# A transformer block on one core: one batch's states loaded and turned ahead of the others, first products over six banks, and a new order of all steps

## The chip, the cores and the metric

The kernel runs on one core of one Trainium2 chip. The metric is the device time of one execution in microseconds (us); several runs are taken and their median is compared. Engines in this text: PE is the matmul engine (TensorE), DVE is VectorE, ACT is ScalarE, POOL is GpSimd, SP is SyncE, which here only issues DMAs.

## What is computed

Two blocks follow each other. The first is a block-recurrent cross attention between tokens `x` and states:

```python
# x: (B=8, H=8, S=512, D=64), state: (8, 8, Ns=32, 64)
scores  = scale * x @ state^T            # (8, 8, 512, 32)
xread   = softmax(scores) @ state        # (8, 8, 512, 64)
scores2 = scale * state @ x^T            # (8, 8, 32, 512)
sread   = softmax(scores2) @ x           # (8, 8, 32, 64)
attn    = concatenate([xread, sread], axis=2)      # (8, 8, 544, 64)
# the second block: attn as 4352 rows of 512
h  = attn_rows @ w_in                    # (4352, 2048)
sp = maximum(h, 0) + log1p(exp(-abs(h)))           # softplus
out = (h * erf(sp)) @ w_out              # (4352, 512)
```

`x` and `state` are float32. The two weights are read as pairs of 32-bit words (float64) and are turned into float32 on the chip.

## The kernel before

**Tiling.** Batches are worked one after the other, each with its 512 tokens, in two passes over the hidden width: pass A takes the first half of `d_ff` (1024 columns) and the first half of both weights, pass B the second half. The rows that come from the states (`sread`) of all batches are done together between the passes ("SA", "SB"). The hidden layer is not taken from `xread`: for each batch the states are multiplied with `w_in` first (`mixed`, steps A1m, A2m, ...; for the first batch `mixed_part`, steps n00 to n12), and the softmax weights `y` are multiplied with that product. From the second batch on, these products and those with `w_out` are done with seven products in place of eight, with sums on DVE (`hidden`, `chain`, `second_twice`, `inner`).

**The first batch** has steps of its own: `attention0` (x0 to x3 turn x on PE, s0 turns its states, q0 and q1 are its scores, tm, max, less, exp, sum, inv, norm, ta are the first softmax in two halves, big, wt, wz, wn, tw the second one, rd0 and rt0 read x with it), and `first_unit` (first products h0 to h7, each of 512 columns, with ACT's softplus h0s and copy h0c, an error function for two of them, h0e, a product on DVE, h0g; then second products o00 to o36, where the first digit is the group of rows and the second the pair of k). h0 to h7 go to PSUM banks k modulo 3; the second products to banks 3 + r modulo 3. PSUM has eight banks; scores, turned tiles and `mixed` use banks 6 and 7, `mixed` also 1 and 2.

**The other batches** go through `attention(b)`: x is loaded in a turned layout by sixteen loads of 64 KB (a1xq0 to a1xq7, two each), turned on DVE (a1tx), the scores (a1s) are sixteen products into banks 6 and 7, copied by ACT (a1c0, a1c1), and so on to y (a1ta). `sums_y(b)` makes y's sums on DVE (y11 to y14); A1f01 and what follows are the hidden products of `chain`.

**The states of batches 1 to 7** are loaded by POOL: a POOL copy ("hold", L486) waits for the first batch's softmax weights, and eight DMAs (`load_st`, L360, steps lst1 to lst8, one for each head) follow it. Two steps u0 and u1 (`turn_states`, L1041) turn them on PE, four and three tiles of 128 by 128, into banks that `attention0` used, and DVE copies them back (u0c, u1c). Everything that uses `st` stands behind that.

**The weights.** `w_in` comes in pieces i0 to i3 (two 512 KB loads each), `w_out` in o0 to o3; each is converted by two passes on ACT (a0, a1) and two on DVE (v0, v1).

**The order.** Every piece of work is a named step. A long string, `ORDER`, lists all names (2511 of them before) in the order in which they are issued, and `in_order` adds a dependency between each instruction and the one before it on the same engine. So each engine, and each DMA queue (SP's, POOL's), works strictly in the order of that string. An entry such as `~6*19` stands for 19 filler products into bank 6, which keep PE at work while it has nothing else:

```python
        if name[0] == "~":
            k, n = name[1:].split("*")
            issue(name, lambda: warm(bank[int(k)][:, 0:P], int(n)))
        else:
            issue(name, do.pop(name) if ORDER.split() else do[name])
    in_order(begun)
```

**Lines of the profile.** L423 fillers, L441 turning of x, L448 of the first states, L456 scores, L461 four turned tiles (tm, ta, tw), L945 n00 to n12, L956 h0 to h7, L977 second products of the first batch, L524 and L534 rd and rt, L549 a1s, L638 A1m, L687 hidden products, L740 and L810 second products, L238, L239, L240 DVE's add, subtract and multiply, L246 copies and other steps that are called with arguments.

Of the kernel before, what the change touches and what calls it, by code (L numbers as in the profile page):

```python
# [20 lines left out]
warm lx0 lx1 lst0 lx2 lx3 i0l0 i1l1 i1l0 i0l1 x0 x1 x0c i2l0 s0 x1c x2 s0c i2l1 q0 x2c x3 q00c  # L21
i3l1 q01c i0a0 big0 tm0 x3c i0v0 i0a1 q1 i3l0 max0 q10c i0v1 q11c less0 a1xq6 ~7*5 tm1 i1a1 big1
n00 max1 exp0 i0+a0 less1 sum0 exp1 a1xq2 n00c0 sum1 i0+a1 i1a0 inv0 inv1 norm1 i2a0 norm0 hold
~6*19 ta1 i1v0 lst1 i2a1 ta0 n00c1 lst6 i0+v0 i1v1 lst3 ta1c lst2 ta0c i0+v1 lst7 i3a0 o1l0 ~0*6
n02 i2v0 lst4 n01 big n02c0 lst8 i2v1 i3a1 ~2*3 h0 lst5 n01c1 o0l1 n01c0 i3v0 wt0 o0l0 n02c1 n10
wt1 a1xq3 i3v1 h1 n10c0 o1l1 n10c1 a1xq0 y01 wz n12 h0s wn1 h0c u1 n12c1 h1s u0 u1c n12c0 h1c wn0
a1xq4 tw1 y02 u0c tw0 h0e a1xq1 h2 tw1c h0g a1xq5 tw0c o0a0 rd0 a1xq7 o1a0 o0v0 o3l0 h4 rn0 y04
o1v0 yl0 a1tx1 rt0 o3l1 h3 h2s a1tx0 h2c a1tx2 o1a1 a1tx3 h5 o0a1 o1v1 rc0 h4c o0v1 a1s h4s h3c h7
T1 h3s a2xq4 a1c0 a1c1 t01 o2l0 a1tu0 h5c a2xq3 h6 h5s a1my0 h7c t0k a1mx0 h7s a2xq1 a1tu1 o10 h6s
a1my1 a2xq0 a1mx1 a2xq2 A1m a1sb0 h2e t31 a1x0 a1sb1 a2xq7 h2g o20 a1ex0 a1x2 t02 a1ex1 a1sm0 a1x1  # L30
A1m10 o22 o2l1 a1sm1 A1m01 A1m11 a1iz y03 a1ey0 a1nm0 o12 a1nm1 A1m00 h6c a1ta0 o3a0 A1M1 A1f01
a1ta1 a1ey1 o00 y11 A1M2 A1f0c y12 a1ty0 A1f06 a1ty1 h4e A1f02 y13 a1kz A1M3 A1f0u2 a1x3 A1f05 y14
o2a1 a2xq6 h4g A1f07 o2a0 a2xq5 o02 t32 A1M4 A1f0u3 o2v0 A1f0c11 A1f0c22 A1f04 h6e o3v0 a1z0 A1f11
o3a1 a1z3 o2v1 a1z1 A1f03 a1z2 A1f0c21 yl1 a2tx0 o04 A1f1c o3v1 A1f16 A1f0c12 A1f0s12 A1f12 T2
A1f0s22 A1f1u2 rd1 A1f0s21 t11 a1iy A1f0s11 t04 A1f17 h6g a2x3 rn10 rn11 A1f1c11 rt1 A1f15 A1f1u3
t34 rc1 T4 A1f14 o24 A1f1c22 A1e0 t61 a2tx2 A1f13 t21 t41 a2s A1f1c12 A1f1s22 t22 o06 A1g0 A1f1s11
a3xq1 a2c1 t1k A1f1c21 o14 a2c0 A1f1s12 a2tu0 o0c A1f1s21 o16 o0d t12 a2mx0 a2x2 a3xq7 A1e1 a2my0
o30 t3k yk0 a2sb0 a3xq5 o26 a3xq2 A1g1 a2ex0 a3xq0 A2m a3xq4 a2sm0 a2x0 o32 A2m00 t62 a3xq3 a2iz
A2m10 t42 a2nm0 A2m11 t2k o2c o34 a3xq6 a2ey0 A2M1 A2m01 a2ta0 a2x1 a2ey1 o36 A2M2 y21 A1q A2f01
o3c A2f05 A2f0c a2ty0 o1c y22 A1ap50 A1A1 A2f06 y23 A1ap10 a2ty1 A2f0u2 A2M3 A2f02 a2kz a2iy y24  # L40
A2f07 t24 T3 A1ap11 A2f0u3 A2f0c11 A1A3 A1ap51 A1ac A2f04 A2f0c22 A2M4 A2f11 A2f0c21 a2z3 t33 t4k
A2f03 t03 A2f1c a2z2 t51 a2z0 a3tx2 A1ap20 a2z1 yk1 A2f16 A2f0c12 o2d A2f0s12 o3d A1A2 A2f12
A2f1u2 o1d A2f0s22 yl2 A2f15 t13 yk2 A2f1c11 t23 A2f17 t6k a3tx0 rd2 A2f1u3 A1A4 A2f14 rn21 a3x2
rn20 t52 A1b2 rt2 A1ap21 rc2 A2f1c22 a3s A1ac11 A1a2 A2f13 a3c0 a4xq3 t43 t64 A2f1c21 A1ap60 A1a3
a3c1 a4xq2 A1ap61 A2f1c12 a3x0 A1bp10 t5k a3tu0 A1au2 a4xq0 A2f1s12 A1bp11 A2f0s21 t14 A1ap70 a3x1
a3mx0 A2f1s21 a3x3 A1ap71 A2f1s11 a4xq6 A1a4 A2f1s22 A3m A2f0s11 a4xq7 t44 A1au3 a3sb0 a4xq5
A1ap40 A1ac22 a3ex0 A1ap41 a3my0 A1ap30 A1ac21 t63 a3sm0 A1bc A1ap31 A3m01 A3m11 A1bp60 A1b3 a3ey1
A1bp61 a3iz A1ac12 A3m10 A1bp20 a3ey0 a3nm0 A1d2 A1bp50 A1bu2 a4xq4 A3m00 t53 A1bp51 a3ta0 A1bp21
A1bp70 t54 A2e0 y31 A1bp71 A3M1 A3f01 a3ty1 A3f05 a3ty0 A1bu3 A3f0c A3M2 A1bp40 a3kz A2e1 y32
# [1101 lines left out]
```

## Time and profile before

| | |
|---|---|
| median of 3 runs | 689.32 us (688.62 to 690.2) |
| the profiled execution, its own time | 691.2 us |
| its span, first to last instruction | 689.1 us |
| mean granted TensorE clock | 0.994 |
| PE busy | 678.0 us (98%), 5569 instructions |
| DVE busy | 590.7 us (86%) |
| ACT busy | 489.5 us (71%) |
| POOL busy | 89.0 us (13%) |
| DMA | 87.15 MB, mean 126 GB/s |

The span is what the instructions of the core take in that one execution; its own time also holds what lies around them. Times in the trace count from the span's start. Busy times of engines overlap. A granted clock of 0.5 means that PE ran at half speed.

### The profile page before, as it was taken

The numbers are of one execution on the slowest core, as the hardware profiler recorded it, in microseconds if no ns is written. First come the engines' busy times: TensorE is split into PE (matmuls) and PEld (weight loads), VectorE is DVE, ScalarE is ACT, GpSimd is POOL, SyncE is SP. The second block draws the span as 40 slices with busy tenths as digits, with TensorE's granted clock in tenths as the row PEclk, the third lists the DMA queues.
The fourth block names the chain that finished last, engine by engine and source line by source line (L and its number), as shares of the span: only waits on it lengthen the run. The fifth ranks groups of instructions, "written<-read, shape, count | busy, mean of one in ns | idle before, by whom it ended". The sixth has DMA issues, their size and how long they took to land.

```text
span 689.1 us, 13808 instructions
## 1 busy us (share of the span) xinstructions
PE 678.0 (98%) x5569; PEld 588.7 (85%) x5569; DVE 590.7 (86%) x771; ACT 489.5 (71%) x763; POOL 89.0 (13%) x84
## 2 busy tenths in 40 slices
PE   9799999999999999999999999999999999999997
PEld 7436568989898898899998879898989898998996
DVE  6689999999999999999986689787968795968784
ACT  5799967968787776876785795757586838676721
POOL 0300000030021202020201012010202011101112
PEclk9899999999999999999999999999999999999999
DMA  9967367578779977696797335142323315141427
GB/s 297 208 166 181 95 160 232 144 113 194 171 119 245 158 176 134 146 258 139 177 237 170 89 86 71 68 65 53 46 70 44 72 17 100 18 68 16 78 54 123
DMA packets 145567, 87.15 MB, mean 126 GB/s; under 512 B 92512, under 2 KB 137824, under 8 KB 145504
## 3 DMA queue, kind: packets, MB, share of 16 engines
q1 hardware_dynamic: 126448, 67.72, 36.0%
q0 software_dynamic: 18512, 18.03, 20.9%
q8 instruction: 44, 0.72, 0.4%
q10 hardware_dynamic: 544, 0.52, 0.2%
q14 instruction: 19, 0.16, 0.1%
HBM read 46.14 MB, written 40.11 MB: 125 GB/s over the span
## 4 chain that ended last, share of the span: by engine, by line
PE 94%; DVE 2%; DMA 2%; ACT 1%; POOL 1%; issue 0%; DVEq 0%
PE b L810 47%; PE b L687 27%; PE b L740 5%; PE b L638 4%; PE b L1017 4%; PE b L977 3%; PE b L956 2%; DMA st<-in_state_dram 1%; PE b L524 1%; PE b L549 1%; POOL st L360 1%; DMA big<-in_x_dram 1%; PE b L1041 0%; PE b L461 0%; DVE ring L239 0%; DVE z L574 0%
## 5 line engine op out<-in xcount | busy, mean ns | idle before, releaser
L718 POOL DMA_DIRECT2D out_dram<-res x67 | 80.1, 1330 | 572.6 <-DVE res L238 179.7
L810 PE MATMUL b<-big,ring 128*128 128x128 f32 x1196 | 151.4, 275 | 0.0
L810 PEld LDWEIGHTS b<-big,ring 128*128 128x128 f32 x1196 | 144.9, 192 | 4.0 <-ACT res L246 1.0
L246 ACT COPY ring<-b 128x512 f32<-128x512 f32 (+1 forms) x144 | 82.7, 584 | 89.4 <-PE b L687 64.8
L687 PE MATMUL b<-y,m 128*128 128x256 f32 x480 | 121.3, 381 | 0.2 <-DVE y L246 0.2
L246 ACT COPY res<-b 128x512 f32<-128x512 f32 (+2 forms) x125 | 64.4, 524 | 53.9 <-PE b L810 37.3
L687 PEld LDWEIGHTS b<-y,m 128*128 128x128 f32 x480 | 86.5, 190 | 12.9 <-ACT ring L246 1.5
L687 PE MATMUL b<-sy,m 128*128 128x256 f32 x360 | 91.9, 380 | 0.0
L240 DVE TENSOR_TENSOR ring<-ring 128x2048 f32<-128x2048 f32 (+1 forms) x36 | 77.8, 2166 | 9.3 <-ACT ring L695 8.2
L676 ACT ACTIVATE ring<-ring 128x512 f32<-128x512 f32 x128 | 77.0, 632 | 1.0 <-DVE ring L238 0.5
L687 PEld LDWEIGHTS b<-sy,m 128*128 128x128 f32 x360 | 65.0, 190 | 9.0 <-issue 1.1
L810 PEld LDWEIGHTS b<-ta,ring 128*128 128x128 f32 x548 | 67.8, 192 | 5.5 <-issue 3.4
L810 PEld LDWEIGHTS b<-big,ta 128*128 128x128 f32 x572 | 68.9, 192 | 3.4 <-ACT res L246 1.7
L810 PE MATMUL b<-big,ta 128*128 128x128 f32 x572 | 71.8, 275 | 0.0
L810 PE MATMUL b<-ta,ring 128*128 128x128 f32 x548 | 71.8, 276 | 0.0
L239 DVE TENSOR_TENSOR ring<-ring 128x1024 f32<-128x1024 f32 (+3 forms) x66 | 68.8, 1046 | 0.1
L238 DVE TENSOR_TENSOR ring<-ring,b 128x512 f32<-128x512 f32 (+1 forms) x72 | 47.1, 658 | 25.3 <-PE b L687 8.7
L695 ACT ACTIVATE ring<-ring 128x2048 f32<-128x2048 f32 x30 | 57.4, 1913 | 0.2
L238 DVE TENSOR_TENSOR res<-res,b 128x512 f32<-128x512 f32 (+2 forms) x60 | 35.9, 599 | 24.2 <-PE b L810 14.3
L246 ACT COPY b<-b 128x512 f32<-128x512 f32 (+2 forms) x63 | 34.4, 548 | 16.6 <-PE b L810 12.3
L238 DVE TENSOR_TENSOR res<-res 128x512 f32<-128x512 f32 (+1 forms) x56 | 42.0, 751 | 0.8
L238 DVE TENSOR_TENSOR ring<-ring 128x1024 f32<-128x1024 f32 (+1 forms) x35 | 39.8, 1141 | 0.2
(143 smaller groups left out, 972.0 us busy)
## 6 DMA issues: line engine op xcount, KB each, us to landing
out_dram<-res POOLq DMA_DIRECT2D x63, 256.0 KB, 4.8
out_dram<-res SPq DMA_DIRECT2D x32, 256.0 KB, 3.0
big<-in_x_dram SPq DMA_DIRECT2D x30, 256.0 KB, 4.1
big<-in_x_dram SPq DMA_DIRECT2D x112, 64.0 KB, 3.1
big<-in_moe_w_in_dram SPq DMA_DIRECT2D x12, 512.0 KB, 5.4
...
```

What stands on the lines that cost most here:

```text
L238: add = lambda o, a, b: tt(o, a, b, op=ALU.add)
L239: sub = lambda o, a, b: tt(o, a, b, op=ALU.subtract)
L240: mul = lambda o, a, b: tt(o, a, b, op=ALU.mult)
L246: do[name] = lambda: f(*args)
L638: pe.matmul(out=to[j][k][Ns * p:Ns * p + Ns, :], lhsT=by, rhs=w_in[r, 4 * j:4 * j + 4, i, :], start=True, stop=True)
L676: act.activation(out=o, in_=i, func=ACTF.Softplus)
L687: pe.matmul(out=to[:, i], lhsT=xs[n - 1][:, q:q + P], rhs=ys[n - 1], start=(start and i == 0), stop=(i == 1), skip_group_check=True)
L695: step(u + "e%d" % o, lambda s=s: act.activation(out=s, in_=s, func=ACTF.Erf))
L718: nc.gpsimd.dma_start(out=to, in_=of, accum_op=ALU.add)
L740: pe.matmul(out=to[:, E2 * h:E2 * h + E2], lhsT=a[:, k // 2, k % 2], rhs=rhs[n][:, k], start=(start and h == 0 and k == 0), stop=(k == 3), ...
L810: pe.matmul(out=out_[:, P * j:P * j + P], lhsT=lhs[:, i], rhs=rhs[:, i], start=(start and j == 0 and i == 0), stop=(i == 1), skip_group_ch ...
L1017: pe.matmul(out=to[:, P * i:P * i + P], lhsT=xs[n - 1][:, i, k], rhs=ys[n - 1][:, k], start=(start and i == 0 and k == 0), stop=(k == 1), ...
```

## The change

Four edits and a new order.

- The states of the second batch (b = 1) get a load of their own on SP (`load_st1`, step ls1, 64 KB), and are turned by four products of 64 columns into bank 2 (step ub), with a copy on DVE (ubc).
- The eight loads on POOL take the states of batches 2 to 7 only. Their "hold" is now made from the copied scores of the second batch (a1c0). They are turned by u0 and u1 (three tiles each, into banks 6 and 7), which stand among the steps of the second batch's hidden layer.
- h0 to h7 go to banks k modulo 6 in place of k modulo 3.
- `ORDER` is a new list of 2515 names, from its start to its end. The fillers are 4, 12, 9, 2 and 2 in place of 5, 19, 6 and 3.

The code, without the list:

```diff
     def load_st(h):
         i, e = h // 2, h % 2
-        nc.gpsimd.dma_start(out=st[Ns * i:Ns * i + Ns, 1:B, D * e:D * e + D],
-                            in_=state[1:B, h].rearrange("b n d -> n b d"))
+        nc.gpsimd.dma_start(out=st[Ns * i:Ns * i + Ns, 2:B, D * e:D * e + D],
+                            in_=state[2:B, h].rearrange("b n d -> n b d"))
+
+    def load_st1():
+        nc.sync.dma_start(out=st[:, 0].rearrange("p (g d) -> p g d", g=2),
+                          in_=state[1].rearrange("(g h) n d -> (h n) g d", g=2))
...
-        step("hold", lambda: nc.gpsimd.tensor_copy(out=sn[:, 0, 0:1], in_=A0[:, 1, 0, 0, 0:1]))
-        for h in range(H):
-            step("lst%d" % (h + 1), load_st, h)
...
+        if b == 1:
+            step("hold", lambda: nc.gpsimd.tensor_copy(out=sn[:, 0, 0:1], in_=sc[:, 0, 0:1]))
...
-                to = bank[k % 3]
+                to = bank[k % 6]
...
-    for k, bs in enumerate((range(1, 5), range(5, B))):
-        def turn_states(bs=bs, k=k):
-            for n, b in enumerate(bs):
-                pe.transpose(out=o_bank[2 + k][:, P * n:P * n + P], in_=st[:, b, :],
-                             identity=ident)
-        step("u%d" % k, turn_states)
-        step("u%dc" % k, dve.tensor_copy, st[:, bs[0]:bs[-1] + 1].rearrange("p b t -> p (b t)"),
-             o_bank[2 + k][:, 0:P * len(bs)])
+    step("ls1", load_st1)
+
+    def turn_st1():
+        by = ident.rearrange("p (a e n) -> p e a n", a=2, e=2)
+        for g in range(2):
+            for e in range(2):
+                pe.matmul(out=bank[2][D * e:D * e + D, D * g:D * g + D],
+                          lhsT=st[:, 0, D * g:D * g + D], rhs=by[:, e], start=True, stop=True)
+    step("ub", turn_st1)
+    step("ubc", dve.tensor_copy, st[:, 1], bank[2][:, 0:P])
...
+    for h in range(H):
+        step("lst%d" % (h + 1), load_st, h)
+    for k, bs in enumerate((range(2, 5), range(5, B))):
+        def turn_states(bs=bs, k=k):
+            for n, b in enumerate(bs):
+                pe.transpose(out=bank[6 + k][:, P * n:P * n + P], in_=st[:, b, :],
+                             identity=ident)
+        step("u%d" % k, turn_states)
+        step("u%dc" % k, dve.tensor_copy, st[:, bs[0]:bs[-1] + 1].rearrange("p b t -> p (b t)"),
+             bank[6 + k][:, 0:P * len(bs)])
```

The opening of the list, up to the second batch's first hidden product, before:

```
warm lx0 lx1 lst0 lx2 lx3 i0l0 i1l1 i1l0 i0l1 x0 x1 x0c i2l0 s0 x1c x2 s0c i2l1 q0 x2c x3 q00c
i3l1 q01c i0a0 big0 tm0 x3c i0v0 i0a1 q1 i3l0 max0 q10c i0v1 q11c less0 a1xq6 ~7*5 tm1 i1a1 big1
n00 max1 exp0 i0+a0 less1 sum0 exp1 a1xq2 n00c0 sum1 i0+a1 i1a0 inv0 inv1 norm1 i2a0 norm0 hold
~6*19 ta1 i1v0 lst1 i2a1 ta0 n00c1 lst6 i0+v0 i1v1 lst3 ta1c lst2 ta0c i0+v1 lst7 i3a0 o1l0 ~0*6
n02 i2v0 lst4 n01 big n02c0 lst8 i2v1 i3a1 ~2*3 h0 lst5 n01c1 o0l1 n01c0 i3v0 wt0 o0l0 n02c1 n10
wt1 a1xq3 i3v1 h1 n10c0 o1l1 n10c1 a1xq0 y01 wz n12 h0s wn1 h0c u1 n12c1 h1s u0 u1c n12c0 h1c wn0
a1xq4 tw1 y02 u0c tw0 h0e a1xq1 h2 tw1c h0g a1xq5 tw0c o0a0 rd0 a1xq7 o1a0 o0v0 o3l0 h4 rn0 y04
o1v0 yl0 a1tx1 rt0 o3l1 h3 h2s a1tx0 h2c a1tx2 o1a1 a1tx3 h5 o0a1 o1v1 rc0 h4c o0v1 a1s h4s h3c h7
T1 h3s a2xq4 a1c0 a1c1 t01 o2l0 a1tu0 h5c a2xq3 h6 h5s a1my0 h7c t0k a1mx0 h7s a2xq1 a1tu1 o10 h6s
a1my1 a2xq0 a1mx1 a2xq2 A1m a1sb0 h2e t31 a1x0 a1sb1 a2xq7 h2g o20 a1ex0 a1x2 t02 a1ex1 a1sm0 a1x1
```

and after:

```
warm lx0 lst0 lx1 lx2 lx3 i0l0 i0l1 i1l0 i1l1 x0 s0 x1 s0c x0c i2l1 x2 x1c q0 x2c i2l0 x3 q01c
q00c i0a0 big0 tm0 ls1 x3c i0v0 i0a1 max0 q1 i0v1 q11c i3l1 q10c less0 i0+a0 ~7*4 n00 tm1 big1
exp0 i0+v0 i3l0 i0+a1 sum0 big i1a0 inv0 max1 a1xq5 norm0 i1a1 less1 ~6*12 ta0 i1v0 exp1 a1xq4
n00c1 n00c0 sum1 ta0c wt0 inv1 norm1 i2a1 ~7*9 ub i1v1 ta1 i2a0 a1xq1 i0+v1 n02 ta1c i2v0 a1xq0
n02c0 ~6*2 n01 wt1 i2v1 h0 a1xq6 n01c0 i3a0 n01c1 o1l1 wz n02c1 n10 o0l1 i3a1 i3v0 o0l0 h1 n10c1
a1xq7 n10c0 i3v1 h0c o1l0 a1xq3 y01 ~7*2 n12 wn0 h0s h5 y02 h1c n12c1 a1tx2 n12c0 h1s wn1 tw0
a1tx0 tw1 ubc a1xq2 h0e h3 o2l0 tw0c h0g o2l1 tw1c o3l1 o0a0 rd0 a1tx3 y04 o0a1 o0v0 h4 a1x1 rn0
yl0 o1a0 o0v1 rt0 o1a1 h2 o1v0 a1tx1 rc0 o1v1 a1s h5s t01 h7 T1 h5c a2xq2 a1c1 a1c0 o3l0 t02 h3c
t31 a2xq6 h6 hold a1tu0 h3s lst7 h2c a1mx0 lst4 h7c a1tu1 o20 lst1 h4s t32 a2xq1 h7s lst5 a1sb0
h6s a1mx1 a2xq5 lst8 h2s o00 a1my1 lst2 t04 y03 lst3 h2e t34 A1m yk0 a1sb1 lst6 a1x3 h2g t3k a1x2
```

More of the change, by code (lines that the diff above doesn't have):

```diff
@@ L20 @@
 ORDER = """
[L21 to L49, printed above, removed]
@@ new lines @@
+t31 a2xq6 h6 hold a1tu0 h3s lst7 h2c a1mx0 lst4 h7c a1tu1 o20 lst1 h4s t32 a2xq1 h7s lst5 a1sb0
+h6s a1mx1 a2xq5 lst8 h2s o00 a1my1 lst2 t04 y03 lst3 h2e t34 A1m yk0 a1sb1 lst6 a1x3 h2g t3k a1x2
+a1ex1 a1my0 o02 a1ex0 a1sm1 h4c a1sm0 h6c o10 A1m11 a1iz a1nm1 A1m00 A1m10 a2xq3 a1nm0 a1ey0 o22
+a1ta1 a1ey1 a1ta0 a1x0 A1M1 o2a0 A1f01 y11 a1ty1 A1m01 A1f05 a1ty0 A1f0c o2a1 o12 A1M2 a1kz y12
+a2xq0 y13 A1M4 t0k A1f06 o2v0 h4e u0 A1M3 y14 A1f02 A1f0u2 a1iy h4g o3a0 A1f07 A1f0c11 o2v1 u1
+A1f0u3 A1f11 a1z1 o3a1 A1f0c22 a1z0 A1f04 a1z3 o3v0 h6e a1z2 a2tx0 A1f03 yk1 a2xq4 A1f0c21 o24
@@ new lines @@
+o3v1 A1f1c a2xq7 A1f0c12 A1f16 t1k u0c A1f0s22 T2 A1f12 A1f1u2 A1f0s21 A1f17 h6g A1f1c11 A1f0s11
+rd1 A1f0s12 u1c t11 A1f1u3 A1f15 T4 a2x3 rn11 rn10 rt1 A1f14 t12 t2k t61 A1e0 o04 a2x2 A1f1c22 t41
+a2tx2 A1f13 rc1 A1f1c21 A1g0 a2s o06 A1f1s12 a3xq1 a2c0 A1f1c12 a2c1 a3xq5 t14 A1f1s22 o26 t21
+a2tu0 o0c a3xq0 A1f1s11 a2x1 A1f1s21 t33 o14 a2mx0 a2x0 yl1 a2my0 A1e1 o16 a3xq6 a2sb0 a3xq7 o30
+A1g1 a3xq3 a2ex0 A2m a3xq2 a2ey0 a2sm0 o0d o2c a2ey1 t42 o2d o32 a2iz A2m10 t22 a2nm0 A2m11 A2m00
+o34 A2m01 a2iy a2ta0 A2M1 A2f01 y21 A2M2 o36 A2f0c y22 a2ty0 a2ty1 A2f06 o3c t13 a2kz A2M3 A2f02
@@ new lines @@
+A2f0u2 t23 y23 A2f05 A2f0c11 A1q o1c A2f07 o1d A2M4 A1ap10 a3xq4 A2f0u3 t03 t62 A2f11 y24 t6k
+A2f0c22 A2f04 A1A1 A2f03 a2z1 A2f0c21 a2z0 a3tx0 A1ap50 A2f1c a2z3 a2z2 t4k A2f16 t44 A1A2 o3d
+A1ap51 A2f1u2 A2f0c12 A2f12 T3 A2f17 A2f1c11 a3tx2 A2f15 A2f1u3 A1ap11 t24 t51 t64 A2f14 A2f0s12
+A2f1c22 A2f0s11 rd2 t43 A1a2 A1ac A2f13 rn21 a3x2 rn20 A1A4 rt2 A1ap60 rc2 A1A3 a3s A1a3 A1ap61
+a3c0 a4xq7 A2f0s22 A1b2 A1ap20 a4xq0 a3c1 A1a4 A1au2 A1ap21 a4xq1 A2f1s11 A1ap70 A2f1c21 a3tu0
+a3x0 A1ac11 A1ap71 a4xq6 A2f0s21 A2f1c12 A2f1s12 A1bp10 t52 A1au3 a3mx0 A1bp11 A2f1s21 a3x3 A1ap40
@@ new lines @@
+a5xq4 A4M1 A2bc11 A4f01 A2bu2 y41 a4x2 A4M3 A2bp51 a5xq0 A4f0c A4f05 y42 A2b4+ A4M2 A4f02 A2b3
+a4ey1 a4x3 A4f06 A2d3 y43 a4ey0 A2bp70 a4ty1 A2d0 A4f0u2 a4ty0 A2bp71 A2b4 A4f07 a4kz A2bu3 y44
+a5xq3 A4f0c11 A2bp40 A4M4 A4f0u3 a4iy A2bc22 A2bp41 A4f0c22 A4f11 A3g0 A3e1 A4f04 A4f03 A2D0
+A4f0c21 A2bp30 A4f0c12 A4f1c A3g1 A2bp31 a4z1 A2bc21 A4f16 a4z2 a4z3 a4z0 A4f12 A4f1u2 A4f15
+A2bc12 A3q A2d1 A4f17 A2d2 A3ap10 yl4 a5tx2 A4f1u3 A3ap50 A2U2 A4f14 A3A1 A4f0s22 rd4 A4f1c22
+a5tx0 A4f1c21 A3ap11 A2D1 rn40 rn41 rt4 A2U3 A4f13 a5x1 rc4 A4f0s11 A3a2 a5s A3ac A4f1c11 A3A2
@@ new lines @@
+A3ap60 A2D2 a5c0 A4f1s11 A3a3 A3ap61 a5x0 A2D3 a5c1 yk4 A3ap20 A4f1c12 a5tu0 A3ap21 A3au2 A4f0s21
+A3ap70 A3A3 A3ac11 A4f1s22 A3ap71 A4f0s12 a5mx0 A3bp10 A4f1s21 a6xq0 A3au3 A3A4 A3ap51 A4f1s12
+A2D4 a6xq2 A3ap40 a5sb0 A3bp11 a5x2 A3ac22 A5m a5ex0 a6xq3 A3a4 a5sm0 A3ap41 A5m10 A3ap30 A3b2
+A3ac21 A3bc A3ap31 a5iz a5my0 A5m11 A5m00 A3bp60 a5nm0 a5ey1 A3bp61 a6xq6 A3bp20 A3bu2 A3ac12
+a5ey0 A3bp21 a5ta0 a6xq1 A3bp50 a6xq5 A5M1 A3bp51 A4e0 A5f01 y51 a6xq4 A3b3 A5f05 a5x3 y52 a5ty1
+A3bp70 A5m01 a5ty0 A5f0c A3bp71 A5M2 A5f02 a5kz A3bu3 y53 a6xq7 A5M3 A5f06 A5f0c11 A3b4+ A3bp40
@@ new lines @@
+SApc12 SBg o7+a0 B0f16 o7a0 B0f12 B0f1u2 SApc11 B0f15 o7a1 SBA1 o7v0 B0f17 o7+v0 o7+v1 SAp40
+B0f1u3 B0f1c22 o7v1 B0f13 B0f0s12 w04 SBA2 B0f0s22 B0f14 SApc21 B0f1c12 B0f1c11 SBp10 TB1 yL1
+B0f1s22 SAd3 B0f1c21 SAd0 SAd2 TB2 B0f1s12 B1m yK2 SBpc SAd1 B0f0s21 w31 B0f1s21 w32 w03 SBp20 TB3
+B1m11 B1m00 B1m10 TB4 w5k B0f0s11 B1f01 w4k B1m01 B1M1 SBp60 w2k B1f0c w3k SBpc11 B1M2 B0f1s11
+SBd0 SBA4 B1f02 w41 B1M4 B1f05 B0e0 B1M3 B1f06 w51 SBA3 SBp50 w42 B1f0c11 B0g0 SBpu2 B0e1 B1f11
+SBp70 w11 B1f0u2 B0g1 B1f07 SBpu3 B0ap10 B1f0u3 SBpc22 B0q SBd3 SBp30 B0A1 B1f04 SBpc12 B0ap11
@@ new lines @@
+B1f0c22 w43 B1f0c21 B1f03 w21 w12 B1f1c B0a2 SBp40 B0A2 B1f16 SBpc21 w34 B0ac SBd2 B0ap50 w62
+B1f1u2 w33 w14 SBd1 B0ap20 w63 B1f0c12 A7D4 B0ap60 w53 B1f0s11 B0A3 B1f17 B1f12 w22 B1f1u3 w13 w44
+B1f0s22 B0ap21 A7U3 B1f0s12 w52 B1f15 A7D3 B0A4 B0ap51 B1f1c22 B1f14 B0a3 B0ap61 B1f1c21 yL2 w54
+B0ac11 A7D2 B1f13 B0b2 B1f1c11 B0au2 B0bp10 w23 yK3 B1f1s12 B0a4 B0bp11 B1f1s11 B0ap70 B1f1c12
+B0ap71 B0b3 B1f1s21 B1f0s21 B2m w64 w24 B1f1s22 B0au3 B0ac22 B0ap40 B2m11 B2m00 B0ap41 B2m10
+B0ap30 B2M1 B0ac21 B2M2 B0bc B0ap31 B0bp20 B0ac12 B1e0 B0bp21 B0C11 B0bp60 B0b4 B0d0 B0bp61 B2f01
@@ new lines @@
+B1g0 B0bu2 B1e1 B0bp70 B0bp71 B0bp50 B0bu3 B2m01 B0bp51 B0bc11 B0bp40 B2f0c B0bc22 B2M3 B0bp41
+B1g1 B2f02 B2f06 B0bp30 B2f0u2 B1q B0bc21 B0bp31 B2f07 B1A1 B2f05 B2f0u3 B2f0c11 B1ap10 B2M4
+B0bc12 B2f04 B2f0c22 B2f0s11 B2f11 B0U2 B2f0c21 B0U3 B2f03 B2f0s12 B2f1c B0U4 B1ap11 B2f0s22
+B2f0c12 B2f16 B1ac B0C2 B1ap50 B2f1u2 B1a2 B2f0s21 B0d3 B1ap20 B0d2 B1ap21 B1a4 B2f12 B1A3 B2f17
+B1A2 B2f15 B2f1u3 B1ap60 B2f1c22 B0C12 B2f14 B2e0 B1A4 B0d1 B2f13 yL3 B1ap51 B2f1c12 yK4 B2f1c11
+B1a3 B1ac11 B1ap61 B2f1c21 B1bp10 B1au2 B1bp11 B1ap70 B2f1s21 B1ap71 B2f1s12 B2f1s11 B3m B1au3
@@ new lines @@
+B1ac22 B2g0 B1ap40 B3m00 B3m10 B1ap41 B2f1s22 B3m11 B3f01 B1b2 B1ac21 B1ap30 B3m01 B3M1 B1bc
+B1ap31 B3M2 B1b4 B1bp20 B2e1 B3M3 B1bp21 B1bp60 B1ac12 B1b3 B1bp61 B3f0c B1bp50 B1bu2 B2g1 B1bp51
+B1bp70 B1bp71 B2q B3f02 B1bu3 B1bc11 B1bp40 B3f0c11 B1C11 B1bp41 B1bc22 B1d0 B3f06 B3M4 B2A1
+B1bp30 B3f0u2 B1bp31 B2a2 B3f05 B3f0s11 B2ap10 B1bc12 B1bc21 B3f07 B1U2 B2A2 B2ap11 B3f0u3 B3f11
+B1U3 B2ac B3f0c22 B3f04 B1U4 B3f03 B3f0c21 B1C2 B2ap50 B3f1c B3f0s22 B2A4 B1d3 B3f16 B3f12 B1d2
+B2A3 B3f1u2 B3f0s12 B2ap20 B2a4 B3f1c11 B2ap60 B3f0c12 B3f17 B1C12 B3f15 B3f1u3 B1d1 B3f0s21
@@ new lines @@
+B5ap40 B7m11 B7m10 B5ap41 B7m00 B5b4 B5ap30 B5ac21 B5b3 B5bc B5ap31 B5bp60 B5ac12 B6e1 B7M1 B5bp61
+B5bp50 B7M2 B7f01 B5bu2 B6g1 B5bp51 B7f0c B5bp70 B7m01 B5bp71 B5bp20 B5bu3 B6q B5bp21 B5bp40
+B5bc11 B6A1 B7f06 B7M3 B5bp41 B7f0u2 B5bc22 B7f02 B5bc21 B7M4 B5bp30 B6a2 B7f0c11 B5bp31 B7f05
+B5bc12 B7f0s11 B6A2 B7f07 B6ap10 B5U2 B7f0u3 B5C11 B7f11 B7f0c22 B5d0 B7f04 B5U3 B7f03 B5U4
+B7f0c21 B6ap11 B7f1c B5C2 B7f0s12 B6ap50 B6ac B7f0c12 B5d3 B7f16 B6A3 B7f0s21 B5d2 B7f15 B7f1u2
+B6a4 B7l1 B7f0s22 B6ap60 B6A4 B6ap61 B7e0 B7f17 B5C12 B7f12 B5d1 B6ap20 B7f1u3 B7f1c22 B7f14 B6a3
@@ new lines @@
+B7f13 B7f1s22 B6au2 B7g0 B6ap21 B7f1c11 B7f1c21 B6ap70 B7f1s12 B6ap71 B6ac11 B7f1c12 B7f1s11
+B6bp10 B6b2 B7f1s21 B6au3 B6ap51 B6bp11 B6ac22 B6ap40 B7e1 B6b3 B6ap41 B7l3 B6ap30 B6ac21 B7g1
+B6ap31 B6bc B6bp60 B6bp61 B6b4 B6bp20 B6bu2 B7q B6bp70 B6bp21 B6ac12 B6bp71 B7A1 B6bc11 B6bp50
+B6bu3 B7k6 B7l2 B6bp51 B7a2 B7k5 B6bp40 B7k4 B6bp41 B6bc22 B7ap10 B7a3 B6bc21 B7ap11 B7A2 B6bp30
+B7ac B7a4 B6bp31 B7ap60 B6bc12 B7ap61 B7A4 B7ap50 B7au2 B6U2 B7ap51 B6C11 B7A3 B6d0 B7ap70 B7ap71
+B6U3 B7ap20 B7au3 B7ac22 B7ap21 B6U4 B7ap30 B7ac11 B6C12 B7ap31 B7q- B6d1 B7ap40 B7ac12 B6C2
@@ L175 @@
+B7ap41 B7p30 B7ac21 B7w5 B7pc B7D0 B7w4 B7p60 B6d3 B7w3 B6d2 B7p61 B7p31 B7pu2 B7w2 B7D1 B7p70
+B7C121 B7C120 B7d11 B7d10 B7p71 B7v30 B7v20 B7d30 B7v31 B7d20 B7v21 B7d31 B7d21
 """
```

203 lines of the change are left out of this document (78 added, 125 removed).

## The prediction

> **What bounds the kernel now.** I read the page first: who is busy, and where TensorE is not.
>
> ```profile
> PE 678.0 (98%) x5569; PEld 588.7 (85%) x5569; DVE 590.7 (86%) x771; ACT 489.5 (71%) x763; POOL 89.0 (13%) x84
> ```
>
> PE lacks 11.1 us of the span. PE's waits say where:
>
> ```profile
> PE b L1041 <- DMA st<-in_state_dram: 4.1, 1, 4.1
> PE b L423 <- PEq L1135: 0.8, 1, 0.8
> PE b L441 <- DMA big<-in_x_dram: 0.5, 1, 0.5
> PE b L945 <- DVE w_in L376: 0.3, 1, 0.3
> PE b L687 <- DVE y L246: 0.2, 1, 0.2
> ```
>
> The reader is to see one large wait. L1041 is `turn_states` (steps u0, u1), waiting for the states of batches 1 to 7. The other four sum to 1.8 us, and some 5 us lie behind PE's last product (it ends at 684.08). The chain of waits shows what was before that wait (start, length, what):
>
> ```profile
> 16.84 0.58 POOL sn L486
> 17.42 3.98 POOL st L360 x6
> 21.39 0.20 issue
> 21.59 0.59 POOL st L360
> 22.18 8.66 DMA st<-in_state_dram
> 30.84 0.14 issue
> 30.98 1.73 PE b L1041 x7
> ```
>
> POOL issues eight loads one after the other; the last one, issued at 22.18, lands 8.66 us later. PE had nothing else queued: in order, u0 stands ahead of everything. What it cost is more than the wait (window: length, PE busy, PEld, DVE, ACT, POOL, granted clock, DMA share, GB/s):
>
> ```profile
> 26.00:28.00 2.00, 0.88 (x17) 0.18 (x16) 0.56 (x2) 1.99 (x6) 0.00 (x0) 1.00 1.29 186
> 28.00:30.00 2.00, 0.00 (x0) 0.00 (x0) 0.00 (x0) 1.97 (x3) 0.00 (x0) 0.86 0.99 257
> 30.00:32.00 2.00, 1.02 (x5) 1.05 (x6) 0.11 (x1) 0.80 (x1) 0.00 (x0) 0.50 0.46 83
> 32.00:36.00 4.00, 4.00 (x15) 2.97 (x14) 2.90 (x5) 2.14 (x4) 0.00 (x0) 0.50 0.60 97
> 36.00:40.00 4.00, 4.00 (x72) 2.11 (x71) 2.48 (x6) 3.97 (x6) 0.00 (x0) 0.97 0.63 178
> 100.00:300.00 200.00, 200.00 (x1885) 176.52 (x1887) 195.80 (x251) 149.87 (x245) 25.50 (x21) 1.00 0.76 170
> ```
>
> PE is idle from 26.89. The clock falls to a half at 29.44 (a mean of 0.86 over 28:30 is 0.56 us at half) and is back at 36.24 (0.97 over 36:40 is 0.24 us at half). The last line is for later: from 100 to 300 us PE never waits, but DVE has only 4.2 us in 200 to spare. The same eight transposes at full and at half clock, in the timeline:
>
> ```profile
> 16.94 1.15 PE L461 MATMUL b<-ident,ring 128*128 128x128 f32 x8
> 32.49 1.91 PE L461 MATMUL b<-ident,ring 128*128 128x128 f32 x8
> ```
>
> **The stall that goes.** Wait 4.09 us. Half clock from 30.98 on: 0.5 x 1.02 + 0.5 x 4 + 0.03 x 4 = 2.63 us of full-speed work lost. Together 6.72. By the Trainium skill ("TensorE: Matmul & The Clock Gate", Part 1) the array halves its clock after an idle window of about 3.4 us and is freed by about 3.4 us of work, the window running free of the kernel. Here the half came after 2.55 us and stayed 5.3 us behind the first product; by the rule's 3.4 us the half clock would have cost 1.7 us and the forecast would be 0.9 us later; the measured clock decides.
>
> **The new opening, walked.** Nothing is taken off PE but four fillers (33 become 29; 38 records of 19 fillers took 4.51 us, so 0.9 us in all); ub adds four 64-wide products (the like of L448, eight records in 0.66 with its drain; between 0.1 and 0.66, I take 0.3, half of that row for half the width). All else moves, so I walk the new order with before's durations; every time of the new kernel below is an estimate from those rows.
>
> Up to h0 DVE sets the pace in both kernels (busy 5.81 of 6 us in 20:26). The first half's softmax now runs ahead of the second's, so ta0 goes at 15.5 (16.94 with ta1 before); norm1 ends at 18.5, ta1 at 19.2. ACT copies ta1 behind wt0 (0.71) and two halves of i2 (1.07 each), to 20.6; i1v1 ends at 19.7 as before, n02 and n01 follow to 21.3. So h0 starts at 21.3 (before 21.80); one more 0.6 step of DVE in the way would give 21.9.
>
> Then on PE, with 1.72 for each first product h (four records, 1.98 with the drain): h0 to 23.05, n10 0.6, h1 to 25.4, two fillers 0.45, n12 (i3's conversion ends at 25.4: not late) to 26.5, h5 to 28.2, tw0 and tw1 1.0, h3 to 30.95. rd0 needs both copies of tw on ACT: h0's erf ends at 30.2, two copies of 0.5, so 31.2: a wait of 0.25. rd0 1.05, h4, rt0, h2 to 35.85, A1's scores to 36.9, h7 and h6 to 40.35. Before, the last h ended at 48.27. The lead is 7.9, less u0 and u1, which are still owed (7 took 1.73 at half clock, so 6 take 0.75): 7.15. The other way: 6.72 + 0.9 + (-0.3) + (-0.25) = 7.07. I take 7.1.
>
> Each wait that the moves add, with its cover:
> - ls1 on SP, 64 KB ahead of i3: at the 350 GB/s of 4 to 18 us it delays i3 by 0.2; ACT takes i3 at 21.8, 1.4 us after the landing.
> - A1's scores (step a1s) come at 35.85 instead of 43.53. They need ubc (DVE 28.9) and sixteen 64 KB loads of x, turned. The ten that stand ahead of the w_out loads go out as SP's ring empties; in before such loads landed 0.3 apart. I get 25 for the tenth, 29.3 for three w_out loads at 1.5 each, 32.6 for the last. Its turn is at 35.15 in DVE's order, done 35.8: just in time, with 2.5 us of spare on the landing. Late, it would hold h7, h6 on PE and a1c1 with ten steps behind it on ACT.
> - hold now waits for a1c0 (ACT, 39.0); POOL then issues the eight loads as before, 0.6 + 5.8, to 45.4; with the same 3 to 8.7 us of landing 54.1 at the latest. Nothing else is on POOL before 100 us. u0 is reached at about 56.3: 2 us of cover. u0c and u1c (0.47 each) come on DVE at 64.5 and 67, ahead of rd1 and rt1 in banks 6 and 7.
> - Six banks free h3 to h7 from the copies of the h three earlier, but banks 3 to 5 are also those of the second products: o10 waits for h4's copy (ACT, 48.4).
> - SP: the first load of A1's natural x waits for rd0; behind it are y's store, A2's x and o3l0, wanted at 57. Covered.
>
> What is late next is ACT. From 30.2: tw copies 1.0, four w_out halves 4.3, rc0 0.2, table 1.28, twelve copies and softplus 6.2, table 1.28, h2's erf 1.06, so 45.5; then DVE's product h2g 1.13, so 46.65. PE comes from h6 over o20, o00 (3.44) and A1m (1.86) to o02, which needs h2g, at 45.7: it waits 0.95. Below that it costs nothing if PE is later; above, each late ACT step is another 0.5. Then o02, o10, o22 to 51.85, and A1f01 finds its y at 51.45. Behind it ACT is full (15.4 of 17 us in 40:57), and h4's erf with its table stands ahead of u2 of the first chain: f07 waits 0.35, f11 0.25. Bounds for these give-backs: 0 and 3; I take 1.5. At rd1 the walk stands at 66.35 with one A1 product more done than before's 71.31: 71.31 - 66.35 + 0.86 = 5.8 ahead. DVE is about 6.0 ahead at A1f01 (57.36 against 51.95 and 0.66 more done), so its stretch of 100 to 300 us starts earlier too. Behind that PE's work is the same, PE was never idle, and the tail steps are the same: nothing more to gain.
>
> Gain 7.1 - 1.5 = 5.6: span 689.1 to 683.5. The profiled execution took 691.2 itself (2.1 around its span) against the median of 689.32, so I apply the difference to the median: 683.7.
>
> **Rivals.**
> (a) The gain is partly given back where DVE is full. All steps were put in a new order, not the opening alone. For: 4.2 us to spare in 200. Against: DVE's own lead of 6.0, and PE idle 0.0 there before. If the new order doubles DVE's idle time there, PE waits 4.2: 687.9. Between the forecast and that: 685.5 to 687.9.
> (b) Slower: A1's scores. The wait of L1041 is replaced by one for x, 16 loads, earlier in the kernel. For: in before the last of these landed at 37.11, and one issue on SP hung 4.21 us at 26.30 behind full rings. Against: the POOL loads that shared the engines then (w_out loads 2.5 to 4 us apart instead of 1.5) are gone from there. A landing at 37.1 costs 2 us (685.7). A wait over 2.55 us also brings the half clock, another 2.6. It decides from a wait of 4.4, a last landing at 39.6: 5.6 + 1.4 used up. At 5.5 us of wait: 683.7 + 5.5 + 2.6 = 691.8. The skill's same section has idle windows as what re-throttles, which agrees with the trace on the price's kind.
> (c) No change: (a) at its worst with a part of (b): 688 to 690.7. That the edit does nothing can be excluded: in the built order u0 stands behind A1's mixing.
>
> **How the numbers follow.** A measurement of this kernel tells 0.2% (1.4 us) from no change. Forecast 0.68 (681.7, with no give-back and h0 0.5 earlier, to 685.5); (a) 0.16; (c) 0.05; slower 0.11, of it 0.07 for (b) and 0.04 for (a) beyond 7 us. Faster is 0.84. The range holds the forecast and (a), 681.7 to 687.9, less a little at each end.
>
> **What would show it.** Right: no wait of PE for the states; clock 1.00 from 6 us to the end; h6 done near 40.4; A1's scores near 36 without a long wait; waits of PE between 31 and 60 us that sum to 1 to 2, for ACT or DVE. Wrong: a wait at A1's scores for DVE's turn over 2 us, a second stretch at half clock, u0 waiting for the states again, or PE waits for DVE spread over 100 to 300 us.

## The result, and the profile after

The changed kernel takes 685.97 us in the median of 6 runs (685.34 to 686.42), before 689.04 (687.66 to 690.67): 3.1 us less by the medians; the ratio, 0.9946 (0.9929 to 0.9964), is 3.7 us of 689.04. The kernel is faster, as forecast, and its time lies inside the stated range. It does not lie in the part that the forecast itself was given (681.7 to 685.5, around 683.7), but in the part of rival (a) (685.5 to 687.9). The profiled execution took 685.9, its span is 684.1: 5.0 us under the span of before, where 5.6 was forecast.

The page's first line and PE's waits (waiter, what it waited for, us, times, longest):

```profile
PE 676.2 (99%) x5568; PEld 586.8 (86%) x5568; DVE 591.4 (86%) x772; ACT 490.9 (72%) x764; POOL 87.8 (13%) x84
```

```profile
PE b L427 <- PEq L1150: 0.8, 1, 0.8
PE b L980 <- DVE ring L240: 0.6, 1, 0.6
PE b L948 <- DVE w_in L380: 0.6, 1, 0.6
PE b L465 <- DVE ring L246: 0.4, 1, 0.4
PE b L690 <- DVE y L246: 0.3, 1, 0.3
PE b L460 <- DVE big L246: 0.2, 1, 0.2
```

No DMA is left in the list, and u0 and u1 (now L1064) wait for nothing. The wait of 0.6 at L980 is o02, waiting for h2g. The windows that were idle or at half clock before, and the long stretch:

```profile
30.00:32.00 2.00, 2.00 (x50) 0.96 (x52) 1.34 (x2) 1.95 (x4) 0.00 (x0) 1.00 1.06 264
32.00:36.00 4.00, 4.00 (x42) 1.79 (x30) 3.91 (x7) 3.85 (x5) 0.00 (x0) 1.00 0.93 200
100.00:300.00 200.00, 200.00 (x1871) 177.75 (x1870) 195.63 (x246) 151.34 (x246) 27.93 (x23) 1.00 0.73 162
```

The clock is whole, and in 100:300 PE still never waits though DVE again has only 4.4 us to spare. Four lines of PE's timeline carry the walk: h0, A1's scores, A1m, and the second products from o02 on.

```profile
21.34 1.98 PE L959 MATMUL b<-y,m 128*128 128x512 f32 x4
...
36.12 1.57 PE L550 MATMUL b<-big,st 64*32 64x512 f32 x16
...
44.69 1.95 PE L641 MATMUL b<-w_in,st 64*32 64x512 f32 x32
47.21 5.42 PE L980 MATMUL b<-ta,ring 128*128 128x512 f32 x12 [0.58 <-DVE ring L240]
```

So the trace bears out the forecast within 0.6 us, but the medians moved by 3.1, where the predicted 683.7 is 5.3 below 689.04. The open question was where those 2 us are.

### The profile page after: what moved, and what is told of

Same layout as the page of the kernel before. It is cut to its first block, busy times and chain, and to the rows that moved or that the text cites. A ratio compares the mean times of both kernels' runs of the same rounds, so it can differ in the third digit from the quotient of the medians.

```text
span 684.1 us, 13797 instructions
## 1 busy us (share of the span) xinstructions
PE 676.2 (99%) x5568; PEld 586.8 (86%) x5568; DVE 591.4 (86%) x772; ACT 490.9 (72%) x764; POOL 87.8 (13%) x84
## 4 chain that ended last, share of the span: by engine, by line
PE 88%; ACT 6%; DVE 3%; DMA 1%; issue 1%; SPq 0%; DVEq 0%; ACTq 0%
PE b L813 47%; PE b L690 25%; PE b L743 5%; PE b L1020 4%; PE b L641 4%; DMA big<-in_moe_w_out_dram 1%; ACT ring L679 1%; ACT ring L246 1%; PE b L525 1%; PE b L550 1%; PE b L427 1%; ACT ta L374 0%; ACT L679 0%; ACT ring L974 0%; ACT L575 0%
## 5 line engine op out<-in xcount | busy, mean ns | idle before, releaser
L238 DVE TENSOR_TENSOR ring<-ring 128x1024 f32<-128x1024 f32 (+1 forms) x35 | 39.8, 1141 | 1.0 <-ACT ring L246 0.6
```

What stands on the lines that cost most here:

```text
L238: add = lambda o, a, b: tt(o, a, b, op=ALU.add)
```

## The experiments

Ratios are to the kernel before, run beside each on the same chip; where a gain has two numbers, one is the difference of the medians, the other what the ratio gives. Line numbers of these kernels differ by a few from those above. L1041 is u0 and u1 in before's code.

**e1: before again.** No edit.

> The kernel before, unchanged, against itself. The profiled execution of before (691.2 us, span 689.1) lies above all six of its timed runs (687.66 to 690.67), and the gain of the two profiles (5.0 us of span) is larger than that of the two medians (3.1 us). Theory A, the wait for the states varies from execution to execution, and the profiled one was long: spans of the runs spread over some 3 us, from 686 to 689, and those with the longer span have the lower granted clock (0.994 against 0.997 or more); a second profile shows a wait at L1041 other than 4.09 us. Rival B, the wait is the same in all executions and the 1.9 us of difference lie in what the changed kernel loses outside its trace: all spans at 688.5 to 689.5 with clock 0.994, and the second profile has a wait of 4.0 to 4.2 us again.

Measured: 689.23 us (687.89 to 691.26), ratio 0.9989 (0.9976 to 1.0003). Its profile has a span of 687.0, and these lines in PE's waits and in the windows:

```profile
PE b L1041 <- DMA st<-in_state_dram: 2.8, 1, 2.8
```

```profile
28.00:30.00 2.00, 0.15 (x1) 0.18 (x2) 0.00 (x0) 1.97 (x4) 0.00 (x0) 0.97 1.03 236
30.00:32.00 2.00, 2.00 (x10) 2.00 (x10) 1.25 (x4) 0.96 (x1) 0.00 (x0) 0.50 0.77 127
32.00:34.00 2.00, 2.00 (x8) 1.56 (x8) 1.77 (x3) 1.27 (x3) 0.00 (x0) 0.68 0.67 109
```

The wait is 2.80 in place of 4.09, and the half clock costs 0.5 x 2 + 0.32 x 2 and 0.07 just before (0.14 us at half, from 29.86 on), 1.7 us in place of 2.63. Sum 4.5 against 6.7: 2.2 us less, and the span is 2.1 us shorter. All 80 runs of before that stood beside the experiments, sorted by granted clock, show the same:

| granted clock | runs | mean span, us |
|---|---|---|
| 0.994, 0.995 | 12 | 689.1 |
| 0.996 to 0.998 | 45 | 687.5 |
| 0.999, 1.000 | 23 | 685.8 |

Their median span is 687.4 (685.3 to 689.9). The execution of before that I predicted from, 689.1 at 0.994, was one of the longest. Theory A holds: the stall varies from execution to execution, and the profiled one was long.

The table also says how it varies. Its rows lie 1.6 and 1.7 us apart, and 1.7 is what one stretch of 3.4 us at half clock cost in e1. The three traces of this opening (before, e1, and e4 below) have two, one and one such stretch; span less wait and half clock is 682.4, 682.5 and 682.5 us in them, so the stall accounts for the whole difference between them. The shortest row would then be executions with a wait of some 3.3 us and no half clock. No execution of that row was profiled, so this is not shown.

**e2: fillers in front of the wait.**

```diff
-... u1 n12c1 ...
+... ~2*12 u1 n12c1 ...
```

> Before, with 12 filler products into bank 2 put ahead of u1: PE works on for 2.6 us after n12, so that its idle time before the states land falls from 4.09 to about 1.5 us, while the landing stays where it is. It prices the half clock alone, which the prediction took at 2.63 of the 6.72 us. Theory A: no stretch at half clock, the products behind the states at full speed, and 1.5 to 2.6 us less than before where that execution had the half clock; in the medians 0.5 to 2.5 us, as not every execution of before has it in full. Rival B (the half clock has another cause than the idle time, or its price is hidden behind DVE and ACT): a stretch at half clock again, or none and no gain within 0.7 us.

Measured: 688.43 us against 689.92, ratio 0.9971 (0.9959 to 0.9983), 1.5 to 2.0 us. PE's timeline, the fillers and u1 with u0:

```profile
27.77 2.94 PE L421 MATMUL b<-ident 128*128 128x128 f32 x24
30.55 0.93 PE L1039 MATMUL b<-ident,st 128*128 128x128 f32 x7
```

The seven transposes take 0.93 in place of 1.73: full clock; in this execution the states had landed by the time the fillers ended. PE also came 0.9 us later to the fillers than it came to the wait in before, since h0 had waited 1.2 us for ACT; so this one trace alone does not show what the fillers did. The runs do: none of the six has a granted clock under 0.998, against 56 of the 80 of before. (0.998 can come from the end alone: in e8's trace below the clock is at a half only from 681.76 us on, behind PE's last product.) Twelve products that compute nothing bring about half of what the whole change brings, though executions of before that escape the half clock are shorter still (685.8 against a mean span of 686.3 here). The half clock was a real price of its own. Theory A.

**e3, e3b: the split alone, in the old order.** e3b differs from e3 in where ls1 and ub stand and in the bank of three fillers. (In e3 those fillers overwrite ub's product before it is copied, so the second batch's values are changed, not its instructions; e3b computes all.)

```diff
-                to = bank[k % 6]
+                to = bank[k % 3]
...
-ORDER of the changed kernel
+ORDER of before, with ls1, ub, ubc added and hold, lst1 to lst8, u0, u1, u0c, u1c moved
```

> The split of the states alone: the code of the changed kernel with first products over three banks, in the order of before; only the moved steps are put elsewhere (ls1 after i3l1, ub in front of ta1, ubc after n12c0, hold and the eight loads after a1c1, u0 after A1f06, u1 after A1f02, their copies ahead of rd1). Theory A: the wait for the states goes, but what is late next in the old order is rd0, for ACT's copies of tw (h0's erf ends near 30.8, two copies of 0.5, so rd0 at 31.9 where PE would be ready at 29.8) and then the loads of x for A1's scores, the last of which landed at 37.1: so 2 to 3 us of the 6.7 come back as these waits, and the median gains 1 to 2.5 us, less than the full change. Rival B: the order is worth nothing beyond it, and the median gains 3 us or more, as the full change does. Rival C: the x loads hold the scores for over 2.6 us, the clock halves there, and nothing is gained.

> The split of the states alone in the order of before, as in the study's e3, but with ls1 ahead of i3 on SP (as the full change has it), ub behind n02, where the states have long landed, and the three fillers in bank 4 in place of bank 2. In e3 ub stood in front of ta1 and waited 1.6 us for ls1, and the gain was 1.9 us. Theory A: without that wait the split alone gains 2 to 3 us, and the rest up to the full change is the wait for ACT at rd0 (1.3 us in e3) and what the old order leaves behind it. Rival B: the wait of ub was hidden, and it gains 1.9 us again. Rival C: it gains as much as the full change beside it, within 0.5 us, and the new order is worth nothing.

Measured: e3 688.34 us against 689.92, ratio 0.9973 (0.9963 to 0.9982), 1.6 to 1.9 us, as theory A has it; ub waited 1.6 us for ls1. e3b 687.34 us against 689.13, ratio 0.998 (0.9968 to 0.9992), 1.4 to 1.8 us, and its runs lie within 687.2 and 687.65 but for one. In a span of 685.5 e3b's PE waits name what is late next:

```profile
PE b L523 <- ACT ring L244: 1.3, 1, 1.3
...
PE b L463 <- DVE m L244: 0.6, 1, 0.6
```

rd0 waits for ACT and tw for DVE, 1.9 us, and the scores take 1.81 us in place of 1.09 (e1), 0.7 more. So the split takes the wait and most of its spread away, and the old order gives about 2.6 us back: 4.5 less 2.6 is 1.9, near the 1.4 to 1.8 measured. The 2 to 3 us that theory A expected of e3b did not come. Its ratio is no better than e3's, as rival B has it, though the wait of ub is gone and the profiled span is 0.8 us shorter (685.5 against 686.3); the ratios come from two chips and their intervals overlap, so this stays open.

**e8: the changed kernel again**, beside e3b.

> The changed kernel again, beside more runs of before on one chip, and a second profile of it. Theory A (the wait for the states varied from execution to execution and is gone): its runs spread over about 1 us and not 4, clock 0.998 or more in all, and the median gains 3 to 4.5 us; the second profile has PE's waits of 31 to 60 us again, summing to 1 to 2 us, for DVE or ACT, and none for a DMA. Rival B (it has a varying wait of its own): a spread over 2 us, and a second profile with a wait for x at A1's scores.

Measured: 685.99 us, ratio 0.9953 (0.9938 to 0.9968). The second profile has the same span, 684.1, and the same waits to 0.1 us. Eight of nine spans lie within 683.6 and 684.8, one at 685.4 with clock 0.996. Against e3b it is 1.35 us better: that is what the new order, with the six banks that it needs, is worth. Theory A, with one miss: no run was to have a clock under 0.998, and that one, which was not profiled, makes the spread 1.8 us and not 1.

**e4: six banks alone.**

```diff
-                to = bank[k % 3]
+                to = bank[k % 6]
```

> Before with h0 to h7 over six banks, and nothing else changed. Theory A: in the old order PE is never held by a bank of h (its waits are for the states, for x and 0.2 us for y), so the median stays within 1 us of before. Rival B: ACT's copies hold PE's products unseen, and it gains 1 us or more. Rival C: banks 3 to 5 held by late copies delay u0, u1 or the second products, and it loses 1 us or more.

Measured: 689.85 us against 689.13, ratio 1.0005 (0.999 to 1.002). Theory A: alone it gains nothing; a loss of up to 1.4 us (rival C) is not excluded.

**e9: split, six banks, and h5 moved**, the edit against e3b.

```diff
-                to = bank[k % 3]
+                to = bank[k % 6]
...
-... n12 ... tw1 ... h3 ... h5 ...
+... n12 h5 ... tw1 ... h3 ...
```

> The split in the old order (e3b) with six banks, and one step moved: h5 right behind n12 on PE, ahead of tw, as the changed kernel has it; three banks do not allow that. In e3b PE waited 0.61 us at tw for DVE's n12 and tw copies and 1.29 us at rd0 for ACT. Theory A (PE's order there is what the new order is worth; six banks are what it takes): both waits go, PE stands 1.5 to 1.9 us earlier at A1's scores, the x loads, still in the old order, hold it for less than that, and the kernel comes within 0.7 us of the changed one: ratio to before 0.994 to 0.9965. Rival B (the loads' order is what counts): PE waits at A1's scores for x by what it gained, and the median is that of e3b, ratio 0.9975 to 0.9985. Rival C (ACT, which sets h2's erf and with it o02, hides it): no wait at the scores, but one of 1 to 2 us at the second products for DVE's product behind the erf, and the ratio of e3b again.

Measured: 687.41 us against 689.58, ratio 0.9971 (0.9959 to 0.9983), 2.0 to 2.2 us. That is level with e3b's 687.34, which was measured on another chip; by the ratios it is 0.6 us better, within the intervals of both. The waits of 0.6 at tw and 1.3 at rd0 became these:

```profile
PE b L548 <- DVE big L244: 0.5, 1, 0.5
PE b L548 <- ACT sT L244: 0.5, 1, 0.5
PE b L523 <- ACT ring L244: 0.4, 1, 0.4
```

L548 is the scores, waiting first for DVE's turn of x and then for ACT's rc0, which stands behind the w_out halves. The ratio lies between what theory A and rival B expected, nearer to B, and half of the wait at the scores is ACT's. Moving h5 on PE alone gains 0 to 0.6 us of the 1.35 by these two comparisons: PE arrives earlier and waits there. That the rest comes from moving DVE's, ACT's and SP's lists with PE's is argued from these waits; no run moves those lists alone.

**e7: no split, but the states loaded at the start**, the edit against before.

```diff
-        step("hold", lambda: nc.gpsimd.tensor_copy(out=sn[:, 0, 0:1], in_=A0[:, 1, 0, 0, 0:1]))
...
-warm lx0 lx1 lst0 lx2 lx3 i0l0 ...
+warm lx0 lx1 lst0 lx2 lx3 lst1 lst6 lst3 lst2 lst7 lst4 lst8 lst5 i0l0 ...
```

> Before, with the states of batches 1 to 7 loaded at the start: no hold on POOL, the eight loads are the first thing that POOL issues (from about 1.3 us) and run beside the loads of x and w_in. Theory A: they have landed long before u0 and u1 at 26.9, the wait and the half clock go; the 0.45 MB delay w_in by 1.3 us at 350 GB/s or by up to 2.5, which DVE and ACT, who set the pace up to h0, pass on nearly in full, and after n12 the same waits for ACT and for x come that the split alone has: the median gains 0 to 2.5 us. Rival B: the loads in 256-byte rows hold the start by 4 us or more and the kernel is slower than before. Rival C: their delay is hidden, and the median gains over 3 us, so that no split was needed.

Measured: 689.38 us, ratio 0.9994 (0.9983 to 1.0004). L1041 waits no more and the clock is whole, but the opening is late by what was saved. PE's waits and h0 in its timeline (21.80 before):

```profile
PE b L459 <- DVE ring L238: 1.0, 1, 1.0
PE b L521 <- ACT ring L244: 0.9, 1, 0.9
```

```profile
24.25 1.98 PE L953 MATMUL b<-y,m 128*128 128x512 f32 x4
```

h0 is 2.4 us later, as the last load of w_in is (it lands at 22.6 us, before at 20.2), and rd0 waits 0.9. Theory A. Eight loads beside w_in delay it, and eight loads behind it make u0 late; loading one batch's 64 KB early and the rest later avoids both.

**e5a: x loaded later, behind two more w_out loads**, in the changed kernel.

```diff
-... o1l0 a1xq3 ... a1xq2 ... o2l0 ... o2l1 ...
+... o1l0 ... o2l0 ... o2l1 a1xq3 a1xq2 ...
```

> The changed kernel with the last four x loads of A1 (a1xq3, a1xq2) behind two w_out loads more (o2l0, o2l1) on SP: in the changed kernel's trace those two land at 37.1 and 39.2, so the x loads land near 39 and their turn on DVE ends near 40, where PE comes to A1's scores at 36.1. It makes the wait of the prediction's rival (b) and tests its price. Theory A (in order, a late load costs its wait, and a wait over 2.6 us a stretch at half clock of some 5 us behind it): PE waits 3 to 4 us at the scores, the clock is at a half near 38.7 to 45, and the kernel is 5 to 7 us slower than the changed one, so about 2 us slower than before. Rival B: ACT, which has most work up to 46 us, hides it: a wait of 3 us, but under 2 us lost. Rival C: the wait costs itself, without a half clock: 3 to 4 us.

Measured: 688.13 us, ratio 0.9991 (0.9975 to 1.0007). The scores begin at 36.03 and stop in the middle. PE's wait, the window, the timeline:

```profile
PE b L548 <- DVE big L244: 2.7, 1, 2.7
```

```profile
38.00:40.00 2.00, 0.09 (x1) 0.09 (x3) 0.85 (x2) 0.38 (x1) 0.00 (x0) 1.00 1.04 316
```

```profile
39.91 1.16 PE L548 MATMUL b<-big,st 64*32 64x512 f32 x8 [2.71 <-DVE big L244]
```

The span is 686.8, 2.7 us over the changed kernel's: the wait is paid in full, nothing hides it (against rival B). The median is 2.1 us over the changed kernel's beside it, and not the 5 to 7 of theory A. The clock stays at 1.00, although 2.80 us of idle brought the half clock in e1: rival C in the profile, with a shorter wait than it expected. And the spread is back: ten runs with spans from 685.0 to 688.7, both ends at clock 0.998, so the half clock alone does not explain it. In this kernel as in before, the time varies where a product on PE's path waits for a late DMA.

**e10: 1.4 us of DVE's work moved behind h0**, in the changed kernel.

```diff
-... i0a0 big0 tm0 ... tm1 big1 ... big ... ta0c wt0 ... n01 wt1 ... wz ... ~7*2 n12 ... h5 ...
+... i0a0 tm0 ... tm1 ... ta0c ... i2v1 big0 big1 big ... n10c0 wt0 wt1 i3v1 wz ... h5 n12 ...
```

> The changed kernel with 1.4 us of DVE's work (big0, big1, big) put from before the first softmax's end to behind i2v1, with the exponentials that need it (wt0, wt1) behind n10c0 on ACT, wz behind i3v1, and h5 ahead of n12 in place of two fillers. It asks what is late next. The prediction has DVE set the pace up to h0, and ACT from 30 to 46 us. Theory A: h0 starts 0.8 to 1.4 us earlier (21.3 in the changed kernel), n12 is done earlier still, but ACT's list is as long as before, so rd0 stays near 31 with a wait of 1 to 2 us and o02 stays within 0.5 us of 47.2: the median within 0.7 us of the changed kernel, ratio to before 0.9945 to 0.9965. Rival B: DVE's pace is passed on, o02 comes 1 us or more earlier, and the median gains 1 us more, ratio under 0.994. Rival C: wz and the products behind it come late on DVE, rd0 is past 32, and it loses 0.7 us or more against the changed kernel.

Measured: 687.19 us, ratio 0.9969 (0.9958 to 0.998), 1.1 us over the changed kernel by this ratio and e8's. h0 and o02 on PE, then two copies on ACT:

```profile
20.86 1.98 PE L957 MATMUL b<-y,m 128*128 128x512 f32 x4
...
47.84 5.42 PE L978 MATMUL b<-ta,ring 128*128 128x512 f32 x12 [0.42 <-DVE ring L238]
```

```profile
19.94 0.37 ACT L244 COPY m<-b 128x256 f32<-128x256 f32 x1 [0.54 <-PE b L946]
20.98 0.27 ACT L244 COPY m<-b 128x128 f32<-128x128 f32 x1 [0.66 <-PE b L946]
```

h0 comes 0.5 earlier, o02 0.6 later, and rd0 starts at 32.37, past 32: rival C. Without wt0 and wt1 in between, ACT waits 1.2 us for n02 and n01, and h2's erf starts 0.6 later on it (45.48 against 44.84), since ACT then runs to it without a pause. Up to 46 us the opening of the changed kernel is as long as ACT's list, not DVE's.

## Why the prediction was right, and where it was off

**Direction right, size too large.** The time is inside the range because the range held rival (a) as well. What rival (a) describes, PE waiting where DVE is full, did not happen. That the number fell into its part was luck; the reason is the step below.

**The wait that goes: mechanism right.** The wait for the states and the half clock are gone (PE's waits of after), the half clock is a price of its own (e2), six banks alone bring no gain (e4), and the split alone brings 1.4 to 1.8 us (e3b), the new order the rest (e8).

**The step that was off: "I apply the difference to the median".** The profiled execution of before was 691.2 against a median of 689.32; I saw that and put the difference down to nothing. It belonged to the very term that I was pricing: the stall was 6.72 in that execution and 4.5 in e1's, whose span of 687.0 is close to the median of 687.4. With 4.5 in place of 6.72 the same sum gives 5.6 - 2.2 = 3.4, and 3.1 to 3.7 was measured. The stall varied from execution to execution; the trace shows one draw of it.

**The half clock.** I let the measured stretch (5.3 us behind the first product) stand against the rule of the Trainium skill ("TensorE: Matmul & The Clock Gate", Part 1) of about 3.4 us. In e1 the half lasted 0.07 / 0.5 + 2 + 1.28 = 3.4 us and cost 1.7, just the rule's figure. Both occur. The free-running window of about 3.4 us in that section of the Trainium skill fits them: one window in e1, two in the trace of before.

Why e5a's 2.71 us cost no clock and e1's 2.80 did can be worked out from the moments at which the clock changes in the traces. In before these are 29.45, 36.27 and 688.22 us, which is 2 and 191 times 3.413 apart; in e1 29.86, 33.28 and 685.22, 1 and 191 times. So the clock changed only on a grid of 3.413 us, which stands elsewhere in each execution. In e5a's trace the one change is at 684.14, after PE's last product; 189 steps back the grid has a point at 39.02, inside the wait of 37.20 to 39.91. So 1.82 us of idle lie before that point and 0.89 behind it. In e1 all 2.80 us lie between two points (26.45 and 29.86), in e4 2.72 of 3.17, in before 2.55 of 4.09. The stretches with 2.55 us of idle or more were followed by a half, the one with 1.82 was not. The limit between them is not known, and no run moved a wait of one length over the grid. My "a wait over 2.55 us also brings the half clock", in rival (b), does not hold as a rule: e5a's 2.71 brought none.

**The walk of the opening.** h0 forecast 21.3, measured 21.34; A1's scores 35.85 and 36.12; h6's end 40.35 and 41.16; o02 46.65 with a wait of 0.95, and 47.21 with 0.58. The 0.8 at h6 is the scores: they ran 1.57 us in place of 1.09 and started 0.27 late. The last x load landed at 34.8 (forecast 32.6), but its turn on DVE came at 35.56 (forecast 35.15), behind steps that had kept DVE busy since 31.88, where it had waited 0.29 us for an earlier x load; so the last load itself no longer held it. By the same working as in the prediction the lead is 48.27 - 41.16 - 0.75 = 6.4 in place of 7.1, and the give-backs are 6.4 - 4.9 = 1.5, as taken. My second way to 7.1 was no check of the first: it counts four fillers as 0.9 us of PE's time, but those in front of h0 fill time in which PE has nothing else to do, and h0 came only 0.46 earlier. The waits of 0.35 and 0.25 forecast for f07 and f11 did not come, and PE's waits from 31 to 60 us sum to 0.6, not to 1 to 2. PE's last product ends 4.9 us earlier than in before's trace, against 5.6.

**Covers that held.** The last load of i3 landed at 20.67 (20.21 before; 0.2 of delay was forecast for ls1), and ACT took it at 21.61 without a wait; the eight loads on POOL, issued from 39.8 to 44.5, landed by 49.4, and u0 went at 56.83; DVE's full stretch gave nothing back, against rival (a).

**Rival (b)** did not happen, but e5a shows its place and one half of its price: 2.7 us for 2.7 of wait. The other half, the clock, was not paid. The wait of 4.4 us from which it was to decide was not tried.
